# Output tiles in groups of 4, 1 and 4, and another listed order, in chunk attention followed by token mixing

## The chip, the cores and the metric

The kernel runs on one core of a Trainium2 chip. Its engines are PE (TensorE, matrix products), DVE (VectorE), ACT (ScalarE), POOL (GpSimd) and SP (SyncE); the DMA engines move data between device memory and the on-chip SBUF. PE writes to PSUM, which has 8 banks of 512 float32 columns here. The metric is the device time of one execution in microseconds (us), lower is better.

## The reference

`q`, `k` and `v` are 8 batches x 8 heads x 576 rows x 64 columns, float32. The attention is local: rows in chunks of 64, each chunk attends only to itself.

```
scores = q_c @ k_c.T / 8              # 64 x 64 for each of 8 * 8 * 9 = 576 chunks
attn   = exp(scores - max) / sum
x      = (attn @ v_c), heads side by side     # 8 x 576 x 512
wq, wk = x @ w_q, x @ w_k             # 8 x 576 x 64
mixed  = (wq @ wk.T / 8) @ x          # per batch, 576 x 576 never needed as such
out    = relu(mixed) @ w_out          # 8 x 576 x 512, float32
```

The kernel works in float16 and uses `(wq @ wk.T) @ x = wq @ (wk.T @ x)`, so that the middle is a 64 x 512 matrix G of each batch.

## The kernel before

One long list, `ORDER` (lines 17 to 45), says in which order everything is issued. A word is a step, a number (unit, batch or tile), for some a part behind a dot, the PSUM bank behind `@`, and the engine behind `:` (A for ACT, D for DVE, P for POOL). The loop at line 434 issues the words one after another. Each engine, and each engine's DMA queue, keeps its own words in the order of the list and waits where it needs data or a free buffer; nothing else sets the order. So a word far ahead in the list can hold up what follows it on the same engine and no other.

The work comes in **units** and **batches**. A unit is 32 chunks of `q` and `k`; there are 18, and a batch of 72 chunks takes two and a quarter. The steps of a unit:

- `LDu.q..`, `LDu.k..` (lines 147, 151): loads by POOL's queue, float32 to float16, in pieces. `q13` is one unit's fourth quarter of rows, `q21` the middle half of two units, `k2` the k of two units. In float16 a unit has 256 KB of k and 256 KB of q. `CQg` (159, 161) clears, once, the places of q that no load fills.
- `TRu` (203): DVE transposes q, or q and k. `KNu` makes the other layout of k: with `:D` by a further DVE transpose (207), and then TR takes two slices; with `:P` by a POOL copy (212) of the third slice of TR.
- `SCu` (223): 32 products for the scores; `EXu` (232): ACT's exponential.

The steps of a batch b:

- `LDb.v..` (142): v, in groups of chunks; `v09` is all of it, 576 KB in float16; `v04`, `v49`, `v05` and `v59` are parts.
- `PVb.p` (254), p = 0 to 3: attention times v for two heads, with the sums in a further column. `RNb.p` (266, 267): DVE divides, giving x.
- `XTb.0`, `XTb.1` (277): PE transposes x; `XE` (291, 293) evicts it. `XTb` needs all four RN of the batch.
- `PJb` (303): x times w_q and w_k; `EP` evicts (314, 316), `DU` (320) copies a part to the other half of the partitions.
- `WTb` (325) transposes wk, `EW` (330, 332) evicts; `GMb` (338) forms G, `EG` (348, 350) evicts; `MXb.m` (356), m = 0 to 3, forms wq @ G for half of the rows and half of the columns, `RL` (370, 372) applies the relu into the tile `rmx`.

`rmx` holds two batches side by side: 1152 rows, nine output tiles of 128 rows. `OMn` (397), n = 0 to 35, is the product of one tile with w_out, `OEn` (409, 411) evicts it. `LW` (166) loads w_out, 512 KB, in four DMAs on POOL's queue.

The tiles of a pair are gathered in groups, listed in `HOMES` (376): a group of size s takes s * 128 rows of the pair, and its tile r takes every s-th row, starting at r (line 396), so that each partition holds s whole rows in a line. Only when all rows of a group are mixed can any of its tiles be formed. When the last tile of a group is evicted, one store by SP's queue (415) writes the group. The evicted tiles lie in places of `qk` whose units are transposed by then; the second number of an entry of `HOMES` is that place, of 36.

SP's queue issues the stores in the order in which the list completes the groups. The first store also waits for the last load but one (`after`, line 508), so that loads and stores don't mix for most of the time. `ZZ` (424) is a matmul on constant data, whose result nobody uses; it keeps PE active.

Of the kernel before, what the change touches and what calls it, by code (L numbers as in the profile page):

```python
# [14 lines left out]
PSUM = bass.MemoryType.PSUM  # L15

ORDER = """
CQ7:A CQ1:D MU ZZ1@0 ZZ1@1 ZZ1@2 ZZ1@3 LS LD1.k1 LD1.q13 LD1.q10 CQ2:D CQ0:D MV LD1.q11 TR1 ZZ1@4 ZZ1@5 ZZ1@6 ZZ3@7
ZZ1@0 ZZ1@5 CQ4:A ZZ1@1 CQ6:A CQ3:A CQ5:A KN1:D LD2.q13 LD2.q11 LD2.k1 LD2.q10 TR2 LD0.k1 LI ZZ1@3 SC1@0 ZZ1@7
KN2:D SC2@4 ZZ1@7 ZZ1@3 ZZ1@7 LD0.q11 LD0.q10 LD0.q13 TR0 KN0:D SC0@2 EX1 EX2 LD0.v49 LD3.q23 PV0.3@6 PV0.2@4 RN0.2  # L20
LD0.v04 LD3.q20 EX0 PV0.1@0 RN0.1 PV0.0@2 LY:A ZZ1@4 RN0.0 ZZ3@5 RN0.3 LD3.k2 LD3.q21 XT0.1@3 TR4 XT0.0@7 XE0.0:A
LD5.q20 KN4:D SC4@0 XE0.1:A PJ0@6 EX4 EP0:A ZZ1@2 TR3 KN3:D SC3@2 DU0:D WT0@6 EW0:D LD1.v09 PV1.0@4 RN1.0 EX3
PV1.2@6 GM0@3 RN1.2 PV1.1@4 RN1.1 LD5.q23 PV1.3@0 EG0:A MX0.2@6 RL0.2:A MX0.1@2 RL0.1:A RN1.3 XT1.0@4 XE1.0:A
LD5.q21 XT1.1@5 XE1.1:A MX0.0@2 RL0.0:A MX0.3@0 PJ1@5 RL0.3:A LD5.k2 TR6 KN6:D TR5 KN5:D SC6@2 EP1:A EX6 DU1:D
WT1@7 EW1:D SC5@5 EX5 LD2.v09 PV2.3@0 RN2.3 LW OM1@3 OE1:A PV2.2@6 RN2.2 PV2.0@4 RN2.0 GM1@2 EG1:A PV2.1@0 OM2@3
OE2:A MX1.0@6 MX1.1@4 RL1.1:A RN2.1 LD7.q21 LD7.k2 OM0@2 RL1.0:D XT2.1@0 OE0:A XE2.1:A XT2.0@5 XE2.0:A LD7.q23
LD7.q20 LD9.k2 LD9.q21 LD9.q23 OM5@4 OE5:A MX1.3@2 RL1.3:A MX1.2@6 RL1.2:A TR7 KN7:D SC7@0 LD9.q20 EX7 PJ2@4 OM4@2
OE4:A OM3@6 OE3:A OM8@0 TR8 KN8:D OE8:A LD3.v09 LD11.q10 LD11.q11 EP2:D WT2@4 EW2:A LD12.q23 OM7@2 OE7:A TR9 TR10
SC8@6 PV3.1@3 RN3.1 LD4.v09 LD11.q13 LD11.k1 LD12.q20 PV3.0@0 RN3.0 DU2:P GM2@2 EX8 PV3.3@6 RN3.3 EG2:A MX2.1@2
RL2.1:A PV3.2@4 RN3.2 MX2.3@0 RL2.3:A KN9:P SC9@2 EX9 LD12.q21 MX2.0@6 RL2.0:D LD12.k2 LD14.q20 OM6@0 OE6:D XT3.1@4  # L30
XE3.1:A KN10:P LD14.q23 XT3.0@1 XE3.0:A MX2.2@6 RL2.2:A PV4.0@2 RN4.0 SC10@4 EX10 PJ3@0 EP3:A OM9@6 OE9:A LD14.q21
LD14.k2 TR11 PV4.1@2 RN4.1 PV4.2@4 RN4.2 LD5.v09 DU3:D KN11:P WT3@0 EW3:A OM12@1 GM3@0 LD16.q23 SC11@6 OE12:A
LD16.q20 TR12 EG3:A MX3.0@2 MX3.2@0 EX11 RL3.0:A LD6.v09 OM10@5 RL3.2:A OE10:A PV4.3@6 RN4.3 OM11@4 MX3.1@2 RL3.1:A
MX3.3@0 TR13 KN12:P TR14 SC12@6 LD16.q21 XT4.0@5 XT4.1@2 RL3.3:A OM14@0 OE14:D XE4.0:A XE4.1:A EX12 TR15 OM13@5
OE13:A OM15@2 OE15:A KN13:P OE11:A PJ4@0 EP4:A LD7.v59 PV5.1@6 RN5.1 PV5.0@2 RN5.0 SC13@4 EX13 PV5.2@0 WT4@6 EW4:A
RN5.2 OM16@7 KN14:P PV5.3@2 OE16:A RN5.3 SC14@4 EX14 GM4@6 XT5.0@1 DU4:P EG4:D MX4.1@6 RL4.1:D MX4.3@2 XE5.0:A
MX4.2@4 RL4.2:A OM17@0 OE17:D RL4.3:A KN15:P XT5.1@6 XE5.1:A MX4.0@4 RL4.0:D PV6.1@2 RN6.1 SC15@0 EX15 PV6.0@6
RN6.0 PJ5@4 EP5:A DU5:D OM19@2 OE19:A PV6.3@0 RN6.3 PV6.2@5 LD16.k2 WT5@4 EW5:A OM18@3 LD7.v05 OE18:A GM5@7 EG5:A
RN6.2 XT6.0@2 XE6.0:A TR16 KN16:P MX5.1@6 RL5.1:D MX5.0@0 RL5.0:A XT6.1@3 XE6.1:A OM20@2 MX5.2@0 RL5.2:A OE20:A
MX5.3@5 TR17 KN17:P RL5.3:D SC16@3 EX16 OM22@7 OE22:D PJ6@0 EP6:A PV7.0@4 RN7.0 PV7.1@2 SC17@6 DU6:P RN7.1 EX17  # L40
WT6@0 EW6:A OM23@1 OE23:A PV7.3@6 RN7.3 PV7.2@4 RN7.2 GM6@0 EG6:A OM21@1 OE21:A MX6.2@2 RL6.2:D MX6.1@6 RL6.1:A
XT7.1@4 XE7.1:D XT7.0@1 OM25@0 XE7.0:A PJ7@4 OE25:D OM24@7 EP7:A WT7@3 EW7:D MX6.3@4 RL6.3:D MX6.0@0 RL6.0:A GM7@2
EG7:D OE24:A DU7:D OM28@5 MX7.3@6 OE28:A MX7.1@1 MX7.0@3 OM29@0 OE29:D OM27@5 RL7.3:D OE27:D RL7.1:A RL7.0:A OM30@1
OM31@0 OE31:A OE30:D OM32@5 OE32:D MX7.2@6 RL7.2:A OM26@3 OE26:A OM33@6 OE33:A OM34@4 OE34:A OM35@1 ZZ1@6 OE35:A
""".split()


# [491 lines left out]
```

## Time and profile before

| | |
|---|---|
| median of 3 runs | 119.21 us (117.7 to 119.91) |
| the profiled execution: its own time | 118.41 us |
| its span, first to last instruction | 116.5 us |
| mean granted PE clock | 0.952 |
| busy: PE / DVE / ACT / POOL | 95.2 / 84.7 / 74.4 / 55.7 us |
| loads (POOL's queue) | 14.68 MB written to SBUF |
| output (SP's queue) | 17 stores: 7 of 768 KB, 5 of 512 KB, 5 of 256 KB |

The span is shorter than the execution's time, which has what lies around the first and last instruction too. A granted clock of 1.00 is full speed. A row of a view of groups reads: line, engine, operation, output <- input, shape, count | busy us, mean ns of one | idle time before, and what ended it. A row of the timeline reads: start, length, engine, line, operation, count, and in brackets the idle time before it and what ended that. Matmuls overlap with those ahead and behind, so a row of the chain that ended last (start, length, what) prices a group of matmuls better than the length in the timeline.

### The profile page before, as it was taken

To read this page: it belongs to the slowest core of one execution; us is meant where nothing else is said; L and a number is where in the kernel's file an instruction comes from. 1 tells how busy PE (TensorE), PEld (TensorE's weight loads), DVE (VectorE), ACT (ScalarE), POOL (GpSimd) and SP (SyncE) were. 2 spreads that over 40 slices of the span, in tenths; PEclk is the share of its full clock that TensorE was granted. 3 is DMA by queue.
4 is the path that set the end of the run, shared out by engine and by line. 5 is a ranking of instruction groups with operands and counts; after the bars stand their busy time and mean duration, and the time that the engine had idled before them with its cause. 6 is when DMAs were issued, how large, how long until landed. Compare 5 with 4: busy or idle time off the path is not lost.

```text
span 116.5 us, 3850 instructions
## 1 busy us (share of the span) xinstructions
PE 95.2 (82%) x1648; PEld 53.8 (46%) x1648; DVE 84.7 (73%) x135; ACT 74.4 (64%) x109; POOL 55.7 (48%) x77
## 2 busy tenths in 40 slices
...
GB/s 31 187 177 198 160 172 211 178 168 211 173 176 203 211 214 197 164 182 162 200 213 207 203 165 174 161 179 190 114 264 407 400 407 400 295 191 7 371 385 143
DMA packets 46016, 24.62 MB, mean 211 GB/s; under 512 B 38192, under 2 KB 39216, under 8 KB 46000
## 3 DMA queue, kind: packets, MB, share of 16 engines
q0 software_dynamic: 42912, 14.68, 113.0%
...
q14 instruction: 3, 0.02, 0.1%
...
## 4 chain that ended last, share of the span: by engine, by line
DMA 50%; PE 26%; POOL 9%; DVE 7%; issue 4%; ACT 1%; DVEq 0%; POOLq 0%
DMA vt<-in_v_dram 43%; PE pb L397 13%; DMA qk<-in_k_dram 7%; POOL qk L151 5%; PE pb L303 3%; DVE qkT L203 3%; POOL qk L147 2%; PE pb L338 2%; PE pb L277 2%; PE pb L254 2%; PE pb L356 2%; DVE xn L267 1%; PE pb L223 1%; DVE rmx L370 1%; POOL vt L142 1%
## 5 line engine op out<-in xcount | busy, mean ns | idle before, releaser
L397 PE MATMUL pb<-wout,rmx 128*128 128x512 f16 x144 | 35.7, 380 | 0.1
L203 DVE STREAM_TRANSPOSE qkT<-qk 128x1536 f32<-128x1536 f32 (+2 forms) x20 | 26.9, 1359 | 4.9 <-DMA qk<-in_q_dram 4.8
L267 DVE TENSOR_TENSOR xn<-pb,rec 128x576 f16<-128x576 f32 x32 | 24.2, 757 | 1.3 <-DVE rec L266 0.2
L232 ACT ACTIVATE est<-pb 128x1024 f16<-128x1024 f32 x18 | 18.5, 1026 | 9.9 <-PE pb L223 9.8
L151 POOL DMA_DIRECT2D qk<-in_q_dram x33 | 17.9, 548 | 10.3 <-DMA vt<-in_v_dram 6.0
L411 ACT COPY qk<-pb 128x512 f32<-128x512 f32 x27 | 15.8, 587 | 9.7 <-PE pb L397 9.1
L223 PE MATMUL pb<-qkT,kN 64*64 64x128 f16 x576 | 13.4, 235 | 7.4 <-DVE kN L207 7.3
L397 PEld LDWEIGHTS <-rmx 128*128 128x128 f16 x144 | 13.0, 101 | 13.1 <-DVE rmx L370 0.8
L142 POOL DMA_DIRECT2D vt<-in_v_dram x10 | 16.1, 1612 | 2.6 <-DMA qk<-in_k_dram 2.3
L212 POOL COPY kN<-qkT 128x512 int32<-128x512 int32 x9 | 9.7, 1083 | 14.5 <-DVE qkT L203 12.8
L372 ACT ACTIVATE rmx<-pb 128x576 f16<-128x576 f32 x23 | 14.3, 653 | 3.2 <-PE pb L356 2.2
L223 PEld LDWEIGHTS <-kN 64*64 64x64 f16 x576 | 10.4, 117 | 11.2 <-DVE kN L207 9.6
L293 ACT COPY xT<-pb 128x512 f32<-128x512 f32 (+1 forms) x15 | 9.2, 637 | 7.7 <-PE pb L277 7.6
L277 PE MATMUL pb<-iden,xn 128*128 128x128 f32 x72 | 9.9, 278 | 3.3 <-DVE xn L267 3.3
L266 DVE RECIPROCAL rec<-pb 128x9 f32<-128x9 f32 x32 | 6.8, 213 | 6.5 <-PE pb L254 6.5
L254 PE MATMUL pb<-vt,est 64*64 64x65 f16 x576 | 9.4, 194 | 2.2 <-DMA vt<-in_v_dram 1.8
L424 PE MATMUL pb<-unit 128*128 128x512 f16 x24 | 9.0, 516 | 2.6 <-DVE unit L448 2.6
L303 PE MATMUL pb<-xT,wpj 128*128 128x512 f16 (+1 forms) x64 | 10.4, 308 | 0.5 <-ACT xT L293 0.4
L277 PEld LDWEIGHTS pb<-iden,xn 128*128 128x128 f32 x72 | 7.9, 140 | 5.5 <-issue 2.6
L254 PEld LDWEIGHTS <-est 64*64 64x64 f16 x576 | 7.3, 107 | 5.8 <-ACT est L232 2.4
L207 DVE STREAM_TRANSPOSE kN<-qk 128x512 f32<-128x512 f32 x9 | 9.0, 1004 | 0.0
L409 DVE COPY qk<-pb 128x512 f32<-128x512 f32 x9 | 6.1, 683 | 4.0 <-PE pb L397 4.0
...
## 6 DMA issues: line engine op xcount, KB each, us to landing
...
qk<-in_q_dram POOLq DMA_DIRECT2D x7, 256.0 KB, 9.9
out_dram<-qk SPq DMA_DIRECT2D x5, 256.0 KB, 2.7
qk<-in_k_dram POOLq DMA_DIRECT2D x4, 256.0 KB, 6.0
```

The lines of the kernel that those rows point to most:

```text
L142: d = nc.gpsimd.dma_start(vt[b % NVB][:, lo:hi, 0:D], vb[b, :, lo:hi])
L151: d = nc.gpsimd.dma_start(view[rows, SIDE[i], j : j + n], qt[rows, b : b + n])
L203: nc.vector.transpose(out=to[:, s : s + step], in_=words(view[:, s : s + step, j]))
L223: nc.tensor.matmul(ps[CH * (eta % 2) : CH * (eta % 2) + CH, bank + f, P * g : P * g + P], lhsT=kN[u % NR][rows, CH * eta : CH * eta + CH, ...
L232: nc.scalar.activation(est[u % NR][:].rearrange("p f g k (w r) -> p (f g k) w r", r=R), ps[:, bank : bank + 2].rearrange("p k c -> p (k c) ...
L254: nc.tensor.matmul(ps[CH * o : CH * o + CH, bank + at // 512, at % 512 : at % 512 + D + 1], lhsT=est[u % NR][rows, i // 2, eta // 2, SIDE[i]],
L267: nc.vector.tensor_tensor(out=xn[b % 3][:, :, p], in0=xv[:, :, 0:D], in1=rec[p][:, :, None].broadcast_to([P, NPR, D]), op=ALU.mult,)
L277: nc.tensor.transpose(ps[:, bank + at // 4, P * (at % 4) : P * (at % 4) + P], xn[b % 3][:, i].rearrange("p h c -> p (h c)").bitcast(F32), ...
L303: nc.tensor.matmul(to, lhsT=wpj[:, c, e, :], rhs=rhs, start=(c == 0 and e == 0), stop=(c == 1 and e == 1),)
L372: nc.scalar.activation(dst, src, AF.Relu, scale=scale_moe)
L397: nc.tensor.matmul(ps[:, bank, :], lhsT=c[:, r], rhs=wout[:, i, :], start=(i == 0), stop=(i == NI - 1),)
L411: nc.scalar.copy(os_, ps[:, bank, :])
```

## The change

`HOMES` and `ORDER` change; no function does. In pairs 0 and 1 the groups of output tiles are 4, 1, 4 instead of 3, 3, 3 and 3, 1, 3, 2. A group of four tiles has 512 rows, so the first one of a pair lies within its first batch of 576 rows; the single one spans both batches. In pair 2 they are 2, 2, 1, 2, 2 instead of 2, 2, 2, 2, 1, and in pair 3 they are 2, 2 and five single ones instead of 3, 3 and three single ones. That gives 18 stores: 4 of 1024 KB, 6 of 512 KB, 8 of 256 KB.

The list has the same steps, in another order, with other banks, and on other engines in places: KN is DVE's in 12 units instead of 9, OE in 5 tiles instead of 9, RL in 7 instead of 9, XE in 4 instead of 1, EP in 3 instead of 1, EG in 1 instead of 2, and DU in 2 batches instead of 5 (the rest of KN and DU is POOL's, of the others ACT's). The whole of it:

```diff
@@ -15,33 +15,33 @@
 PSUM = bass.MemoryType.PSUM
 
 ORDER = """
-CQ7:A CQ1:D MU ZZ1@0 ZZ1@1 ZZ1@2 ZZ1@3 LS LD1.k1 LD1.q13 LD1.q10 CQ2:D CQ0:D MV LD1.q11 TR1 ZZ1@4 ZZ1@5 ZZ1@6 ZZ3@7
-ZZ1@0 ZZ1@5 CQ4:A ZZ1@1 CQ6:A CQ3:A CQ5:A KN1:D LD2.q13 LD2.q11 LD2.k1 LD2.q10 TR2 LD0.k1 LI ZZ1@3 SC1@0 ZZ1@7
-KN2:D SC2@4 ZZ1@7 ZZ1@3 ZZ1@7 LD0.q11 LD0.q10 LD0.q13 TR0 KN0:D SC0@2 EX1 EX2 LD0.v49 LD3.q23 PV0.3@6 PV0.2@4 RN0.2
-LD0.v04 LD3.q20 EX0 PV0.1@0 RN0.1 PV0.0@2 LY:A ZZ1@4 RN0.0 ZZ3@5 RN0.3 LD3.k2 LD3.q21 XT0.1@3 TR4 XT0.0@7 XE0.0:A
-LD5.q20 KN4:D SC4@0 XE0.1:A PJ0@6 EX4 EP0:A ZZ1@2 TR3 KN3:D SC3@2 DU0:D WT0@6 EW0:D LD1.v09 PV1.0@4 RN1.0 EX3
-PV1.2@6 GM0@3 RN1.2 PV1.1@4 RN1.1 LD5.q23 PV1.3@0 EG0:A MX0.2@6 RL0.2:A MX0.1@2 RL0.1:A RN1.3 XT1.0@4 XE1.0:A
-LD5.q21 XT1.1@5 XE1.1:A MX0.0@2 RL0.0:A MX0.3@0 PJ1@5 RL0.3:A LD5.k2 TR6 KN6:D TR5 KN5:D SC6@2 EP1:A EX6 DU1:D
-WT1@7 EW1:D SC5@5 EX5 LD2.v09 PV2.3@0 RN2.3 LW OM1@3 OE1:A PV2.2@6 RN2.2 PV2.0@4 RN2.0 GM1@2 EG1:A PV2.1@0 OM2@3
-OE2:A MX1.0@6 MX1.1@4 RL1.1:A RN2.1 LD7.q21 LD7.k2 OM0@2 RL1.0:D XT2.1@0 OE0:A XE2.1:A XT2.0@5 XE2.0:A LD7.q23
-LD7.q20 LD9.k2 LD9.q21 LD9.q23 OM5@4 OE5:A MX1.3@2 RL1.3:A MX1.2@6 RL1.2:A TR7 KN7:D SC7@0 LD9.q20 EX7 PJ2@4 OM4@2
-OE4:A OM3@6 OE3:A OM8@0 TR8 KN8:D OE8:A LD3.v09 LD11.q10 LD11.q11 EP2:D WT2@4 EW2:A LD12.q23 OM7@2 OE7:A TR9 TR10
-SC8@6 PV3.1@3 RN3.1 LD4.v09 LD11.q13 LD11.k1 LD12.q20 PV3.0@0 RN3.0 DU2:P GM2@2 EX8 PV3.3@6 RN3.3 EG2:A MX2.1@2
-RL2.1:A PV3.2@4 RN3.2 MX2.3@0 RL2.3:A KN9:P SC9@2 EX9 LD12.q21 MX2.0@6 RL2.0:D LD12.k2 LD14.q20 OM6@0 OE6:D XT3.1@4
-XE3.1:A KN10:P LD14.q23 XT3.0@1 XE3.0:A MX2.2@6 RL2.2:A PV4.0@2 RN4.0 SC10@4 EX10 PJ3@0 EP3:A OM9@6 OE9:A LD14.q21
-LD14.k2 TR11 PV4.1@2 RN4.1 PV4.2@4 RN4.2 LD5.v09 DU3:D KN11:P WT3@0 EW3:A OM12@1 GM3@0 LD16.q23 SC11@6 OE12:A
-LD16.q20 TR12 EG3:A MX3.0@2 MX3.2@0 EX11 RL3.0:A LD6.v09 OM10@5 RL3.2:A OE10:A PV4.3@6 RN4.3 OM11@4 MX3.1@2 RL3.1:A
-MX3.3@0 TR13 KN12:P TR14 SC12@6 LD16.q21 XT4.0@5 XT4.1@2 RL3.3:A OM14@0 OE14:D XE4.0:A XE4.1:A EX12 TR15 OM13@5
-OE13:A OM15@2 OE15:A KN13:P OE11:A PJ4@0 EP4:A LD7.v59 PV5.1@6 RN5.1 PV5.0@2 RN5.0 SC13@4 EX13 PV5.2@0 WT4@6 EW4:A
-RN5.2 OM16@7 KN14:P PV5.3@2 OE16:A RN5.3 SC14@4 EX14 GM4@6 XT5.0@1 DU4:P EG4:D MX4.1@6 RL4.1:D MX4.3@2 XE5.0:A
-MX4.2@4 RL4.2:A OM17@0 OE17:D RL4.3:A KN15:P XT5.1@6 XE5.1:A MX4.0@4 RL4.0:D PV6.1@2 RN6.1 SC15@0 EX15 PV6.0@6
-RN6.0 PJ5@4 EP5:A DU5:D OM19@2 OE19:A PV6.3@0 RN6.3 PV6.2@5 LD16.k2 WT5@4 EW5:A OM18@3 LD7.v05 OE18:A GM5@7 EG5:A
-RN6.2 XT6.0@2 XE6.0:A TR16 KN16:P MX5.1@6 RL5.1:D MX5.0@0 RL5.0:A XT6.1@3 XE6.1:A OM20@2 MX5.2@0 RL5.2:A OE20:A
-MX5.3@5 TR17 KN17:P RL5.3:D SC16@3 EX16 OM22@7 OE22:D PJ6@0 EP6:A PV7.0@4 RN7.0 PV7.1@2 SC17@6 DU6:P RN7.1 EX17
-WT6@0 EW6:A OM23@1 OE23:A PV7.3@6 RN7.3 PV7.2@4 RN7.2 GM6@0 EG6:A OM21@1 OE21:A MX6.2@2 RL6.2:D MX6.1@6 RL6.1:A
-XT7.1@4 XE7.1:D XT7.0@1 OM25@0 XE7.0:A PJ7@4 OE25:D OM24@7 EP7:A WT7@3 EW7:D MX6.3@4 RL6.3:D MX6.0@0 RL6.0:A GM7@2
-EG7:D OE24:A DU7:D OM28@5 MX7.3@6 OE28:A MX7.1@1 MX7.0@3 OM29@0 OE29:D OM27@5 RL7.3:D OE27:D RL7.1:A RL7.0:A OM30@1
-OM31@0 OE31:A OE30:D OM32@5 OE32:D MX7.2@6 RL7.2:A OM26@3 OE26:A OM33@6 OE33:A OM34@4 OE34:A OM35@1 ZZ1@6 OE35:A
+MU CQ4:A LS LD0.k1 CQ0:D LD0.q10 ZZ1@0 ZZ1@1 ZZ1@2 ZZ1@3 ZZ1@4 CQ7:D LD0.q11 CQ6:D ZZ1@5 LD0.q13 LD1.k1 ZZ1@6 ZZ1@7
+ZZ1@3 ZZ1@6 ZZ1@4 MV ZZ1@2 TR0 KN0:D CQ1:A LD1.q11 LD1.q10 ZZ1@2 CQ2:A CQ3:A LY:A LD1.q13 LD2.q13 ZZ1@2 SC0@4 TR1
+KN1:D ZZ1@0 ZZ1@2 ZZ5@0 SC1@1 LD2.q11 LD2.k1 LD2.q10 TR2 KN2:D SC2@6 LI LD0.v04 EX0 CQ5:A EX1 PV0.0@3 RN0.0 LD0.v49
+PV0.1@2 RN0.1 LD3.q21 LD3.k2 PV0.2@0 RN0.2 ZZ2@4 EX2 ZZ1@4 PV0.3@6 RN0.3 XT0.0@5 XE0.0:A LD3.q20 LD3.q23 TR3 KN3:D
+XT0.1@0 XE0.1:A PJ0@0 EP0:A DU0:D SC3@4 WT0@1 EX3 EW0:D TR4 GM0@3 EG0:A MX0.0@6 MX0.1@2 LD5.q20 MX0.3@0 RL0.0:A
+LD1.v09 MX0.2@4 RL0.2:A PV1.0@6 RL0.3:D KN4:D LW PV1.2@0 RN1.2 RN1.0 SC4@4 RL0.1:A EX4 LD5.q23 PV1.1@2 LD5.q21
+PV1.3@4 OM0@0 RN1.1 OE0:A OM3@6 OE3:A RN1.3 XT1.0@2 XE1.0:A LD5.k2 XT1.1@4 XE1.1:A OM2@3 OE2:A TR5 PJ1@4 EP1:A
+KN5:D SC5@0 EX5 WT1@7 TR6 KN6:D LD2.v09 PV2.1@2 RN2.1 SC6@0 EW1:A PV2.0@5 RN2.0 LD7.q20 GM1@4 LD7.q23 LD7.q21
+LD7.k2 EX6 PV2.3@0 RN2.3 LD9.q20 LD3.v09 PV2.2@2 LD9.q23 DU1:P EG1:A MX1.1@6 RL1.1:A OM1@4 OE1:A RN2.2 MX1.0@0
+RL1.0:A MX1.2@5 RL1.2:A XT2.0@2 XE2.0:A XT2.1@3 XE2.1:A OM4@7 MX1.3@5 RL1.3:A TR7 KN7:D SC7@0 TR8 KN8:D PJ2@3 EP2:D
+OE4:A EX7 OM5@5 OE5:A DU2:D SC8@6 EX8 PV3.0@0 RN3.0 LD9.k2 LD9.q21 PV3.1@2 RN3.1 WT2@4 EW2:A OM7@5 PV3.3@6 RN3.3
+OE7:A GM2@4 EG2:A MX2.0@3 RL2.0:A MX2.1@5 RL2.1:A LD11.q11 LD11.q13 OM6@7 OE6:A PV3.2@2 TR9 LD11.k1 MX2.2@0 MX2.3@4
+RL2.3:A RL2.2:A RN3.2 LD4.v09 OM8@6 LD11.q10 XT3.0@2 XE3.0:A LD12.q20 LD12.q21 LD14.q20 LD12.k2 KN9:P SC9@3 XT3.1@0
+OM12@5 EX9 TR10 XE3.1:A KN10:D OE12:A SC10@2 EX10 OE8:D TR11 PV4.0@0 KN11:D RN4.0 PJ3@6 EP3:A OM9@5 OE9:A WT3@4
+PV4.1@6 RN4.1 LD12.q23 LD14.q23 SC11@2 PV4.2@0 RN4.2 LD14.q21 LD14.k2 LD5.v09 EW3:A GM3@4 EX11 PV4.3@6 DU3:P EG3:A
+MX3.3@4 RL3.3:A MX3.1@2 RL3.1:A OM11@0 OE11:A RN4.3 XT4.1@5 XT4.0@2 XE4.1:A TR12 MX3.2@3 RL3.2:A MX3.0@0 OM10@7
+RL3.0:A LD6.v09 LD16.q23 LD16.k2 OE10:A LD16.q20 XE4.0:D PJ4@5 EP4:A KN12:P SC12@0 EX12 LD16.q21 OM16@3 WT4@5 EW4:A
+TR13 LD7.v59 KN13:P OE16:A OM15@6 OE15:A GM4@2 EG4:A SC13@4 EX13 TR14 DU4:P TR15 KN14:P KN15:P PV5.2@0 RN5.2
+PV5.0@6 RN5.0 OM17@2 OE17:A SC14@3 PV5.1@0 RN5.1 OM14@5 LD7.v05 PV5.3@6 EX14 MX4.1@2 RL4.1:A MX4.3@0 RL4.3:A OM13@4
+RN5.3 OE14:D MX4.0@2 RL4.0:A MX4.2@6 RL4.2:D XT5.1@0 OE13:A XE5.1:D XT5.0@5 XE5.0:A SC15@6 EX15 PV6.1@2 PV6.0@0
+RN6.1 PJ5@4 RN6.0 EP5:A DU5:P OM21@2 OE21:A WT5@4 EW5:A TR16 OM20@0 PV6.3@1 RN6.3 OE20:A PV6.2@5 GM5@3 OM18@4 EG5:A
+MX5.2@0 OE18:A RL5.2:A RN6.2 MX5.0@2 RL5.0:D XT6.1@6 XT6.0@5 XE6.0:A MX5.1@2 RL5.1:A KN16:P SC16@0 EX16 MX5.3@4
+RL5.3:A XE6.1:D PJ6@6 OM22@2 TR17 KN17:D SC17@0 EX17 PV7.0@3 OE22:A EP6:D WT6@6 RN7.0 OM24@5 EW6:D PV7.2@0 DU6:P
+RN7.2 PV7.3@3 RN7.3 OE24:A PV7.1@6 RN7.1 GM6@2 EG6:A OM23@5 OE23:A OM19@2 MX6.0@0 OE19:A RL6.0:D MX6.2@4 XT7.0@6
+XT7.1@2 XE7.1:D RL6.2:A MX6.1@0 RL6.1:D MX6.3@4 OM26@7 XE7.0:A PJ7@2 EP7:D DU7:P OE26:A OM27@7 OE27:D OM28@0 OE28:A
+WT7@2 EW7:D RL6.3:A OM25@7 GM7@2 OM29@0 EG7:D OE25:A MX7.2@3 MX7.3@1 OE29:A RL7.2:D MX7.1@5 RL7.1:D OM30@7 OE30:D
+MX7.0@3 RL7.3:A OM34@1 OE34:D RL7.0:A OM33@4 OE33:A OM31@6 OE31:A OM32@5 OE32:A OM35@3 OE35:A
 """.split()
 
 
@@ -374,10 +374,10 @@
     of = out.rearrange("b s m -> (b s) m")
     ring = words(qk[:])
     HOMES = (
-        ((3, 0), (3, 3), (3, 6)),
-        ((3, 27), (1, 30), (3, 31), (2, 34)),
-        ((2, 9), (2, 11), (2, 13), (2, 15), (1, 17)),
-        ((3, 18), (3, 21), (1, 24), (1, 25), (1, 26)),
+        ((4, 0), (1, 4), (4, 5)),
+        ((4, 27), (1, 31), (4, 32)),
+        ((2, 9), (2, 11), (1, 13), (2, 14), (2, 16)),
+        ((2, 18), (2, 20), (1, 22), (1, 23), (1, 24), (1, 25), (1, 26)),
     )
 
     done = {}
```

## The prediction

> **What bounds the kernel now.** I read the stretches first, then the chain that ended last, then the durations by form. Columns of the stretches: from:to, length, busy time (and instructions) of PE, PEld, DVE, ACT, POOL, then granted clock, DMA share, GB/s.
>
> ```profile
> span 116.5 us, 3850 instructions
> ...
> 12.00:39.00 27.00, 17.34 (x376) 11.14 (x376) 19.73 (x32) 11.44 (x18) 14.10 (x21) 0.81 1.71 185
> 39.00:73.50 34.50, 33.66 (x624) 19.61 (x621) 31.14 (x43) 27.59 (x45) 24.98 (x29) 1.00 1.62 190
> 73.50:86.70 13.20, 12.68 (x317) 8.14 (x317) 10.80 (x22) 9.47 (x15) 3.67 (x4) 1.00 1.71 171
> 86.70:112.80 26.10, 25.50 (x290) 12.52 (x288) 15.75 (x25) 15.50 (x27) 2.80 (x3) 1.00 0.80 318
> ```
>
> From 39 us on, PE is busy 71.84 of 73.8 us. Before that it is not: 17.34 of 27 us, at a mean granted clock of 0.81. So the end is set by how much PE work is left when PE becomes full, and by whatever stops it later. The chain that ended last (start, length, what) names the one thing that does, and also gives PE's price for each word of the list, at full clock:
>
> ```profile
> 19.62 17.21 DMA vt<-in_v_dram
> ...
> 59.64 13.90 DMA vt<-in_v_dram
> ...
> 76.74 0.46 PE pb L223 x32
> 77.20 0.78 PE pb L338 x10
> ...
> 80.64 0.23 PE pb L356 x2
> ...
> 93.11 0.44 PE pb L325 x6
> ...
> 94.41 0.44 PE pb L254 x35
> ...
> 96.95 1.13 PE pb L277 x9
> ...
> 98.09 0.86 PE pb L397 x4
> 98.95 1.02 PE pb L303 x8
> ...
> 112.23 0.58 ACT qk L411
> ```
>
> Prices: SC 0.46, GM 0.78, MX 0.23, WT 0.44, PV 0.23 (35 matmuls are two words), both XT of a batch 1.13, OM 0.86, PJ 1.02. The load issued at 59.64 is v of batch 5 (LD5.v09), landing at 73.54. PE stood for it:
>
> ```profile
> 73.58 0.48 PE L254 MATMUL pb<-vt,est 64*64 64x65 f16 x34 [0.40 <-DMA vt<-in_v_dram]
> ```
>
> And from the DMA views of single stretches, the last load and the last stores (for issues: KB, us to landing; for the queues: start, length):
>
> ```profile
> vt<-in_v_dram POOLq DMA_DIRECT2D x1, 320.0 KB, 10.3
> ...
> 76.43 1.30 POOL L142 DMA_DIRECT2D vt<-in_v_dram  x1
> ...
> 111.97 0.33 SPq L415 DMA_DIRECT2D out_dram<-qk  x1
> ...
> 112.84 0.33 SPq L415 DMA_DIRECT2D out_dram<-qk  x1
> ...
> out_dram<-qk SPq DMA_DIRECT2D x1, 256.0 KB, 2.3
> ```
>
> So PE reaches the list's PV5 just as v5 lands: **the load stream and PE meet at 73.5 us**, which I call the gate. Behind it, PE runs until 112.2, evicts (0.58), stores (issued at 112.84, landed 2.3 later), and closes. The last load, issued at 76.43, lands 10.3 later, at 86.7, and PE still has 25.5 us of work then. Its PV7 stand later in the list, so that load binds nothing.
>
> **The change part by part.** Work is moved, not removed: both lists hold 18 SC, 32 PV, 8 each of PJ, WT, GM, 8 pairs of XT, 32 MX, 36 OM, the same 54 loads, and 24 warming matmuls (ZZ).
>
> *Early part.* Where two lists have the same kinds of work, I compare their reach when the gates open.
>
> ```profile
> 23.24 1.25 DVE L203 STREAM_TRANSPOSE qkT<-qk 128x1024 f32<-128x1024 f32 x1 [1.33 <-DMA qk<-in_q_dram]
> 23.26 1.18 ACT L293 COPY xT<-pb 128x512 f32<-128x512 f32 x2 [4.67 <-PE pb L277]
> 26.46 2.10 PE L303 MATMUL pb<-xT,wpj 128*128 128x512 f16 x8
> 39.97 0.40 PE L397 MATMUL pb<-wout,rmx 128*128 128x512 f16 x1
> ```
>
> Before, the units are taken 1, 2, 0; after, 0, 1, 2. By then 3136 KB of loads must have landed for the fourth unit in either list, so its transpose stays at about 23.2 (summing the loads' sizes in listed order). PJ0 has its input at 23.26 + 1.18 = 24.44 but starts at 26.46, as SC4 stands ahead of it in PE's queue and needs that transpose; after, PJ0 stands ahead of SC3. Batch 0's mixing (PJ, WT, GM, MX) thus starts about 2 us sooner, and the weights wout (LW) are loaded before units 5 and 6 instead of after v2. With four output tiles over the first 512 of batch 0's 576 rows, OM0, OM3 and OM2 can run before batch 1 is mixed. Before, the first OM is at 39.97, behind 7 SC, 9 PV, 2 XT pairs, 2 PJ, 2 WT, 1 GM, 4 MX. After, ahead of SC6, stand 6 SC, the same rest, and 3 OM: 3 x 0.86 - 0.46 = **2.12 us of work gained** if both get there at one time. Against it: LW's 512 KB now delay units 5, 6 and v2. From v2's landing (19.62 + 17.21 = 36.83, after 5312 KB) and the 23.24 above (3136 KB) the stream does 160 KB/us, so they come up to 3.2 us later than before; units 5, 6 had, by the same rate, 36.83 - 576 / 160 = 33.2, so at most 36.4, where the DVE is still busy with batch 1's four RN. I count 0.6 us of loss (between nothing and 1.5): PE's lead is about 1.5 us at 40 us.
>
> Some of the ZZ that stood between 19 and 29 us move ahead of SC1. By the row 12 to 39 the clock is 0.81 there, and PJ0 takes 2.10 us against 1.02 later. If the three OM met that half speed, they would cost 3 x 0.86 more, 2.6 us, and the early lead would be gone; the row from 39 on has 1.00, and OM0 stands behind a dense run of batches 0 and 1, so nothing is my value and 2.6 the other end. [...]
>
> *At the gate.* Loads up to v5 and with it come to 12160 KB in both lists, and the queue stood full (DMA share 1.62 over 39 to 73.5), so it lands at 73.5 again; plus or minus 1, since the order of q pieces differs. Ahead of the first PV5 the old list has 13 SC, 20 PV, 5 XT, 5 PJ, 4 WT, 4 GM, 16 MX, 16 OM. The new one has 14 SC, 20 PV, 5 XT, 5 PJ, 5 WT, 5 GM, 16 MX, 15 OM. The difference: 0.46 + 0.44 + 0.78 - 0.86 = **0.82 us more work ahead of the gate**. Before, PE came 0.4 us ahead of v5; now it comes 0.4 + 1.5 - 0.82 = 1.1 ahead, and waits that long. So of the early gain only 0.82 survives, as less work behind the gate.
>
> *Engines.* Moves between engines, by form:
>
> ```profile
> L267 DVE TENSOR_TENSOR xn<-pb,rec 128x576 f16<-128x576 f32 x32 | 24.2, 757 | 1.3 <-DVE rec L266 0.2
> L203 DVE STREAM_TRANSPOSE qkT<-qk 128x1536 f32<-128x1536 f32 x9 | 15.7, 1759 | 0.0
> L207 DVE STREAM_TRANSPOSE kN<-qk 128x512 f32<-128x512 f32 x9 | 9.0, 1004 | 0.0
> L203 DVE STREAM_TRANSPOSE qkT<-qk 128x1024 f32<-128x1024 f32 x7 | 8.5, 1220 | 3.5 <-DMA qk<-in_q_dram 3.5
> L266 DVE RECIPROCAL rec<-pb 128x9 f32<-128x9 f32 x32 | 6.8, 213 | 6.5 <-PE pb L254 6.5
> L370 DVE TENSOR_SCALAR rmx<-pb 128x576 f16<-128x576 f32 x9 | 6.7, 745 | 0.8 <-PE pb L356 0.8
> L409 DVE COPY qk<-pb 128x512 f32<-128x512 f32 x9 | 6.1, 683 | 4.0 <-PE pb L397 4.0
> L320 DVE COPY wq<-wqk 64x576 f16<-64x576 f16 x5 | 1.6, 327 | 2.1 <-ACT wqk L316 1.9
> L291 DVE COPY xT<-pb 128x640 int32<-128x640 int32 x1 | 0.8, 824 | 0.0
> L314 DVE CAST wqk<-pb 128x576 f16<-128x576 f32 x1 | 0.8, 757 | 0.0
> ...
> L411 ACT COPY qk<-pb 128x512 f32<-128x512 f32 x27 | 15.8, 587 | 9.7 <-PE pb L397 9.1
> L372 ACT ACTIVATE rmx<-pb 128x576 f16<-128x576 f32 x23 | 14.3, 653 | 3.2 <-PE pb L356 2.2
> L293 ACT COPY xT<-pb 128x640 f32<-128x640 f32 x7 | 4.9, 693 | 1.0 <-PE pb L277 1.0
> L316 ACT CAST wqk<-pb 128x576 f16<-128x576 f32 x7 | 4.5, 638 | 3.6 <-PE pb L303 3.6
> ```
>
> DVE: three KN more, 3 x (1.004 + 1.220 - 1.759) = +1.40; four OE less, -2.73; two RL less, -1.49; three XE more, two of them at 0.824 and one at the 512-wide copy's 0.683, +2.33; two EP, +1.51; three DU less, -0.98; one EG less, at most -0.68. In all between -0.6 and 0. ACT: four OE, +2.35; two RL, +1.31; three XE less, about -1.97 (two at 0.693, one at 0.587); two EP less, -1.28; the EG at most +0.59: some +0.4 to +1.0. On POOL three KN copies less and three DU more; it has room (24.98 of 34.5). DVE is nearly as full as PE (31.14 of 34.5), so a neutral sum matters: no new bound, and I take nothing for it.
>
> *Stores.* 17 become 18, the last five tiles each alone. Both lists end in OM, OE, one 256 KB store, so the closing 0.58 + 2.3 and the rest stay.
>
> **Sum.** 118.41 (the profiled execution: span 116.5 and 1.9 around it) - 0.82 = 117.6. The median shown, 119.21, lies 0.8 above that execution, so in its terms **118.4**. Gaps behind the gate: 38.66 us from 73.54 to 112.2, for 81.0 - 43.7 = 37.3 of work by the prices, so 1.3; I keep them.
>
> **Rivals.**
>
> *A: the gate opens early, and the lead is kept.* If the new load order brings v5 at 72 or sooner, PE keeps its lead of 1.5 and the old wait of 0.4 goes: 119.21 - 1.9 = 117.3; with no early loss (2.12) 116.7, and with half of the 1.3 us of gaps gone 116.0. For it: POOL's KN copies stand between fewer of the loads. Against: a full queue is not helped by earlier issue.
>
> *B: slower, by TR16.* In the new list DVE's queue has RN6.1, RN6.0, TR16, RN6.3, RN6.2, and XT6 needs the last. TR16 needs LD16.q21, behind 13760 KB of loads. From 12160 KB at 73.54 and 14336 at 86.7 the stream does 165 KB/us there: 73.54 + 1600 / 165 = 83.2. TR16 and two RN follow before XT6.1: 1.76 + 2 x (0.757 + 0.213) = 3.7, so 86.9. PE reaches XT6.1 some 12.8 us of work behind the gate, at 86.3 to 86.8. So it decides from a landing at about 83.0, and each us later costs one: at the old last landing, 86.7, +3.7 - 0.8, 122.1. Before, TR16 stood behind all of RN6. POOL's KN12 ahead of LD16.q21 speaks for it, the full queue against.
>
> *C: the filler is missing.* Three OM spent early can't cover the evictions between PJ, WT, GM, MX in the batches that follow. Each such batch has EP 0.638 and RL 0.653 and their like uncovered, some 2 us. One is paid by the lead; a second and third give 119.2 + 2 to 3, 121 to 122.
>
> *D: stores in a row.* If each of the five single stores waited for the one ahead, five times the 2.3 of the row would stand behind the first, and most of the tail's OM with them: some +6, 124 to 125. The last store issues 0.87 behind the one ahead of it (112.84 against 111.97) and still lands in 2.3, so they overlap; I hold this for nearly excluded. [...]
>
> *E: no change*, 119.2: the gate's 0.82 is given back in gaps.
>
> **How the numbers follow.** Forecast 0.45 (117.3 to 119.0), A 0.18, B 0.20, C 0.10, D 0.02, E 0.05. 2% of 119.21 is 2.4 us, about what a measurement of this kernel can tell, as its three runs spread from 117.7 to 119.91. Faster by over 2% (under 116.8): over half of A, 0.13. Slower (over 121.6): half of B, C and D, 0.22. Within: 0.65. The range leaves out A's extreme and the worst of B, C, D: 115.9 to 122.0.
>
> **What would show it.** An OM before 36 us; PE idle for some 1.1 us at about 73.5, ended by the v load; the last OM's end at 111.4 instead of 112.2. TR16 waiting for a q load beyond 83 would be B; PE's busy time of 39 to 73.5 falling below 33, C. Wrong would be: v5 landing elsewhere than 72.5 to 74.5, or PE gaps behind the gate over 2 us in all.

## The result, and the profile after

The changed kernel is slower by about 1%.

| | before | after |
|---|---|---|
| median (20 runs each) | 118.47 us | 120.27 us |
| range | 117.68 to 120.41 | 118.62 to 122.93 |
| ratio, 95% interval | | 1.0106 [1.0073, 1.0140] |
| span of the profiled execution | 116.5 us | 117.4 us |
| mean granted PE clock in it | 0.952 | 0.936 |
| last OM's end | 112.23 | 113.46 |

Of the changed kernel's 20 runs, 9 took 120.4 to 122.9 us, eight of them at a mean granted clock under 0.91; the ratio leaves these out, and so is smaller than that of the medians, as the ratios below leave out such runs (7 of 12 each of the changed kernel with OM30 elsewhere and with single tiles, at most a third of any other kernel's).

The stretches of the changed kernel (columns as in the prediction: from:to, length, busy time of PE, PEld, DVE, ACT, POOL, granted clock, DMA share, GB/s):

```profile
12.00:39.00 27.00, 20.02 (x355) 11.58 (x348) 20.07 (x32) 12.68 (x17) 17.01 (x22) 0.78 1.68 180
39.00:73.50 34.50, 32.51 (x659) 19.57 (x658) 29.14 (x42) 28.23 (x46) 21.71 (x28) 1.00 1.63 189
73.50:86.70 13.20, 13.20 (x315) 7.79 (x313) 11.49 (x19) 10.22 (x17) 5.22 (x6) 1.00 1.67 175
```

Before 39 us PE is busy for 2.7 us more than it was, at a lower clock, 0.78. From 39 to 73.5 it is busy for 1.15 us less: it waits there. Single rows tell both. The timeline of PE up to that point:

```profile
24.02 2.08 PE L303 MATMUL pb<-xT,wpj 128*128 128x512 f16 x8 [0.78 <-ACT xT L293]
...
29.65 0.29 PE L356 MATMUL pb<-wqk,g 64*128 64x288 f16 x1 [0.47 <-ACT g L350]
...
33.83 0.35 PE L254 MATMUL pb<-vt,est 64*64 64x65 f16 x18 [1.03 <-ACT est L232]
34.11 3.54 PE L397 MATMUL pb<-wout,rmx 128*128 128x512 f16 x8
37.49 1.15 PE L277 MATMUL pb<-iden,xn 128*128 128x128 f32 x9
...
42.53 0.64 PE L223 MATMUL pb<-qkT,kN 64*64 64x128 f16 x31
```

PJ0 is at 24.02 (26.46 before), the first MX at 29.65, and OM0 at 34.11, all as early as forecast. But the eight matmuls of OM0 and OM3 take 3.38 us from their start to that of XT1 at 37.49, twice the 0.86 per word that the prediction had. SC6, the word by which the prediction counts PE's lead, is at 42.53. The stretches around it show why:

```profile
28.00:34.00 6.00, 3.19 (x122) 2.24 (x122) 5.08 (x10) 3.70 (x6) 3.92 (x5) 1.00 1.20 204
34.00:37.30 3.30, 3.30 (x26) 1.31 (x16) 3.27 (x5) 0.59 (x1) 3.16 (x4) 0.51 2.41 162
```

From 28 to 34 PE is busy for 3.19 of 6 us, with many short waits. Then the clock is 0.51 for 3.3 us, just where the OM that were to be the gain stand.

PE's waits from there to the gate, its total in the view of waits from 39 to 73.5 (engine, what it worked on, what it waited for: total, times, longest), and PE at batch 5's PV:

```profile
PE pb L254 <- ACT est L232: 1.0, 3, 0.5
PE pb L356 <- DVE xn L267: 0.5, 1, 0.5
PE pb L277 <- DVE xn L267: 0.4, 1, 0.4
PE pb L325 <- ACT wqk L316: 0.2, 1, 0.2
...
74.94 0.23 PE L254 MATMUL pb<-vt,est 64*64 64x65 f16 x4
```

That is 2.1 us of waits. (At 55.43, the 0.5 of line 356, the view names DVE, but the eviction of G on ACT, 0.37 us from 55.00, ends just ahead of it.) Before, in the same stretch, there was one wait:

```profile
PE pb L223 <- DVE kN L207: 0.2, 1, 0.2
```

The v5 load lands where it did. Its issue in the timeline, and its time to landing in the DMA view of that microsecond:

```profile
61.24 1.83 POOL L142 DMA_DIRECT2D vt<-in_v_dram  x1
...
vt<-in_v_dram POOLq DMA_DIRECT2D x1, 576.0 KB, 12.5
```

61.24 + 12.5 = 73.74. PE is at its PV at 74.94, without a wait for the load: 1.2 us behind v5, where it had been 0.4 ahead.

Behind the gate, the timelines of PE, ACT and DVE near the end:

```profile
106.38 0.39 PE L397 MATMUL pb<-wout,rmx 128*128 128x512 f16 x1
107.15 1.06 PE L397 MATMUL pb<-wout,rmx 128*128 128x512 f16 x3 [0.39 <-DVE rmx L370]
108.14 0.29 PE L356 MATMUL pb<-wqk,g 64*128 64x288 f16 x1
...
108.95 4.48 PE L397 MATMUL pb<-wout,rmx 128*128 128x512 f16 x20 [0.51 <-ACT rmx L372]
...
106.34 1.42 DVE L370 TENSOR_SCALAR rmx<-pb 128x576 f16<-128x576 f32 x2 [0.87 <-PE pb L356]
...
108.25 1.19 ACT L372 ACTIVATE rmx<-pb 128x576 f16<-128x576 f32 x2 [1.66 <-PE pb L397]
...
113.46 0.59 ACT L411 COPY qk<-pb 128x512 f32<-128x512 f32 x1 [0.28 <-PE pb L397]
```

OM30 (106.38) stops after its first matmul until RL7.2 and RL7.1 have written (DVE, 106.34), and RL7.3 on ACT (108.25) starts only when OM30 is through. Neither is needed for a result: OM30 takes every second one of the rows 256 to 511 of its pair, all of batch 6, and RL7 writes batch 7. The built program has these waits: OM30's second and fourth weight loads wait for RL7.2 and RL7.1 (0.68 and 0.55 us in PEld's timeline, at 107.15 and 107.81), RL7.3 for OM30's last matmul (the 1.66 above). The view of waits from 74.9 to 113.5 has the two weight loads (PEld):

```profile
PEld L397 <- DVE rmx L370: 1.2, 2, 0.7
```

In the kernel before, RL7.1 and RL7.0 wait for their MX alone.

### The profile page after: what moved, and what is told of

Read it like the earlier page. It is cut to its first block, busy times and chain, and to the rows that moved or that the text cites. A ratio compares the mean times of both kernels' runs of the same rounds, so it can differ in the third digit from the quotient of the medians.

```text
span 117.4 us, 3858 instructions
## 1 busy us (share of the span) xinstructions
PE 98.0 (84%) x1648; PEld 54.4 (46%) x1648; DVE 84.9 (72%) x133; ACT 73.8 (63%) x111; POOL 54.3 (46%) x77
## 4 chain that ended last, share of the span: by engine, by line
PE 60%; DMA 12%; DVE 11%; POOL 5%; ACT 5%; issue 3%; DVEq 0%; POOLq 0%; ACTq 0%
PE pb L397 28%; DMA qk<-in_q_dram 12%; PE pb L223 7%; PE pb L277 7%; PE pb L303 7%; PE pb L356 4%; DVE xn L267 4%; PE pb L254 4%; PE pb L338 3%; ACT est L232 3%; PE pb L325 2%; DVE rmx L370 2%; POOL qk L151 2%; DVE kN L207 2%; POOL vt L142 1%
## 5 line engine op out<-in xcount | busy, mean ns | idle before, releaser
L397 PE MATMUL pb<-wout,rmx 128*128 128x512 f16 x144 | 38.1, 395 | 1.0 <-ACT rmx L372 0.5
L203 DVE STREAM_TRANSPOSE qkT<-qk 128x1024 f32<-128x1024 f32 (+2 forms) x20 | 25.3, 1279 | 5.1 <-DMA qk<-in_q_dram 5.1
L411 ACT COPY qk<-pb 128x512 f32<-128x512 f32 x31 | 18.0, 588 | 13.7 <-PE pb L397 13.7
L397 PEld LDWEIGHTS <-rmx 128*128 128x128 f16 x144 | 13.5, 107 | 14.7 <-issue 3.8
L372 ACT ACTIVATE rmx<-pb 128x576 f16<-128x576 f32 x25 | 15.3, 652 | 4.4 <-PE pb L356 2.5
L320 POOL COPY wq<-wqk 64x576 f16<-64x576 f16 x6 | 4.0, 663 | 26.3 <-DVE wqk L314 14.4
L207 DVE STREAM_TRANSPOSE kN<-qk 128x512 f32<-128x512 f32 x12 | 12.2, 1013 | 0.0
L424 PE MATMUL pb<-unit 128*128 128x512 f16 x24 | 9.8, 581 | 1.5 <-DVE unit L448 1.5
L293 ACT COPY xT<-pb 128x512 f32<-128x512 f32 (+1 forms) x12 | 7.4, 637 | 5.1 <-PE pb L277 5.0
L212 POOL COPY kN<-qkT 128x512 int32<-128x512 int32 x6 | 6.5, 1093 | 4.7 <-PE pb L254 3.3
```

Of the source, the lines that this page charges most:

```text
L203: nc.vector.transpose(out=to[:, s : s + step], in_=words(view[:, s : s + step, j]))
L372: nc.scalar.activation(dst, src, AF.Relu, scale=scale_moe)
L397: nc.tensor.matmul(ps[:, bank, :], lhsT=c[:, r], rhs=wout[:, i, :], start=(i == 0), stop=(i == NI - 1),)
L411: nc.scalar.copy(os_, ps[:, bank, :])
```

## The experiments

All ratios are to the kernel before on the same chip, 95% interval behind. Two numbers of a profiled execution are followed through them: the time at which PE starts batch 5's PV (73.58 before, 74.94 after), and the time from there to the last OM's end, "the tail" (112.23 - 73.58 = 38.65 before, 113.46 - 74.94 = 38.52 after).

### Keep the clock up

```diff
-EW0:D TR4 GM0@3 EG0:A MX0.0@6
+EW0:D TR4 ZZ2@7 GM0@3 EG0:A ZZ2@7 MX0.0@6
...
-RN1.2 RN1.0 SC4@4
+RN1.2 RN1.0 ZZ2@5 SC4@4
...
-PV1.1@2 LD5.q21 PV1.3@4
+PV1.1@2 ZZ4@0 LD5.q21 PV1.3@4
```

> The kernel after, with ten more idle matmuls in PE's gaps between 28 and 34 us, so that the clock is not at half speed when the two first output tiles come. If the half clock is what cost the early lead: OM0 and OM3 take 0.86 us each instead of 1.74, PJ1 starts near 37.7 us instead of 39.4, PE reaches PV5 at about the landing of v5 (73.7), and the time falls by 1.2 us to a ratio to before of 0.998 to 1.003. If it is only the place of the output tiles ahead of XT1, and not the clock: less than 0.5 us.

Ratio 1.0058 [1.0021, 1.0095]. The same two stretches, and the timeline of PE:

```profile
28.00:34.00 6.00, 5.51 (x118) 2.79 (x115) 4.86 (x9) 3.77 (x6) 5.44 (x7) 1.00 1.30 201
34.00:37.30 3.30, 3.30 (x37) 2.35 (x37) 3.23 (x7) 1.60 (x4) 1.66 (x2) 1.00 2.33 171
...
34.46 1.92 PE L397 MATMUL pb<-wout,rmx 128*128 128x512 f16 x8
...
73.92 0.23 PE L254 MATMUL pb<-vt,est 64*64 64x65 f16 x4
```

With ten idle matmuls in the waits, the clock holds at 1.00, OM0 and OM3 together take 1.92 instead of 3.54, and PE is at batch 5's PV at 73.92, 1.02 us sooner, though it does more (v5 lands at 60.80 + 12.7 = 73.5). The tail stays at 112.45 - 73.92 = 38.53. So the half clock costs about 0.5% by the runs (1.0106 against 1.0058) and 1.02 us, 0.9%, by these two executions, and is not the whole loss. The two intervals overlap, and 1.0058 lies between the two forecasts: the runs alone leave the size open, from nothing to 1%. That the clock is the cause rests on the rows.

### The three early OM later

Undoes the part that was to give the gain: OM0, OM3 and OM2 go behind GM1, PV2.2 and MX1.3.

```diff
-PV1.3@4 OM0@0 RN1.1 OE0:A OM3@6 OE3:A RN1.3
+PV1.3@4 RN1.1 RN1.3
...
-XE1.1:A OM2@3 OE2:A TR5
+XE1.1:A TR5
...
-LD7.k2 EX6 PV2.3@0
+LD7.k2 OM0@7 EX6 OE0:A PV2.3@0
...
-EG1:A MX1.1@6
+EG1:A OM3@5 OE3:A MX1.1@6
...
-MX1.3@5 RL1.3:A TR7
+MX1.3@5 OM2@2 RL1.3:A OE2:A TR7
```

> The kernel after, with OM0, OM3 and OM2 moved behind GM1, PV2 and MX1.3, so that XT1, PJ1 and SC5 don't stand behind them. If their place is what starved DVE (3.25 us idle before PV2): PJ1 near 36 us, DVE idle under 1.5 us there, the three tiles fill PE's gaps between 42 and 47, and the time falls by 1 to 2 us, ratio 0.995 to 1.003. If only the clock counted, the three tiles are paid later at full speed and the gain is 0 to 0.7 us, ratio 1.005 to 1.011.

Ratio 1.0463 [1.0420, 1.0506], by far the slowest kernel of the study, and outside both forecasts. Two stretches:

```profile
34.00:36.00 2.00, 0.35 (x18) 0.23 (x17) 1.93 (x6) 0.32 (x1) 1.23 (x2) 0.72 2.46 159
36.00:44.00 8.00, 6.67 (x90) 4.76 (x94) 4.20 (x6) 3.31 (x5) 2.03 (x4) 0.50 1.50 194
```

Where the early OM had been, PE is idle for 1.65 of 2 us, and the clock then stays at 0.50 for 8 us. So the early OM, slow as they run, also keep PE at work; without them in this order, far more is lost. The undoing takes more away than the one thing, so it prices the hole, and not the OM.

### OM30 elsewhere in the list

```diff
-EG7:D OE25:A MX7.2@3 MX7.3@1 OE29:A RL7.2:D MX7.1@5 RL7.1:D OM30@7 OE30:D MX7.0@3 RL7.3:A
+EG7:D OE25:A OM30@7 MX7.2@3 MX7.3@1 OE29:A RL7.2:D MX7.1@5 RL7.1:D RL7.3:A OE30:D MX7.0@3
```

> The kernel after, with OM30 ahead of MX7 and of RL7 in the list, nothing else. If the waits of OM30 for batch 7's RL (0.39 us) and of RL7.3 for OM30 (OM34 0.51 us later) are what lengthens the tail: the last OM ends 0.4 to 0.9 us sooner, ratio 1.003 to 1.007. If those waits only hide another one: unchanged at 1.0106.

Ratio 1.0067 [1.0018, 1.0117]. In PE's timeline OM30 runs through, but the next word takes over the wait:

```profile
108.11 0.28 PE L356 MATMUL pb<-wqk,g 64*128 64x288 f16 x1 [0.70 <-DVE rmx L370]
```

MX7.0 needs the bank that RL7.2 empties, and nothing stands between them any more. The tail is 112.86 - 75.03 = 37.83, 0.69 shorter, within the forecast. But the interval takes in nearly the whole way from no gain to the tail's full price, so this run alone settles nothing.

### The groups alone, in the kernel before

The kernel before with the new `HOMES`; its list changes only in that OM3 and OM5 swap places, with their evictions, so that each group is complete in time.

```diff
-((3, 18), (3, 21), (1, 24), (1, 25), (1, 26)),
+((2, 18), (2, 20), (1, 22), (1, 23), (1, 24), (1, 25), (1, 26)),
```

(and the other three pairs as in the change)

> The kernel before, with only the new groups of output tiles (tiles 3 and 5 change places in the list, since tile 5 now needs all of batch 1). If the size and number of the stores have no price of their own, as the prediction took: ratio 0.997 to 1.003. If single stores at the end cost their fixed time in a row: slower by 2 us or more, ratio above 1.015.

Ratio 1.0111 [1.0070, 1.0151]: as much as the whole change, with the old order. PE is at batch 5's PV at 73.63, but the last OM ends at 113.22, a tail of 39.59 for 38.65. ACT's timeline, of this kernel and of the one before:

```profile
105.60 1.19 ACT L372 ACTIVATE rmx<-pb 128x576 f16<-128x576 f32 x2 [1.72 <-PE pb L397]
```

```profile
104.02 1.20 ACT L372 ACTIVATE rmx<-pb 128x576 f16<-128x576 f32 x2
```

RL7.1 and RL7.0 start 1.58 us later, behind OM27, which as part of a group of two lies in rows 0 to 255 of its pair, batch 6 again. On PE, OM30 then stands for them:

```profile
106.30 0.38 PE L397 MATMUL pb<-wout,rmx 128*128 128x512 f16 x1 [0.74 <-ACT rmx L372]
...
106.85 2.55 PE L397 MATMUL pb<-wout,rmx 128*128 128x512 f16 x11 [0.17 <-ACT rmx L372]
```

These two waits, 0.91 us, are the tail's 0.94. In this execution the span also ends 5.3 us behind the last OM's end, for 4.3 before; what makes that was not followed up.

### Only pair 3's groups: of three, or single

Two kernels, each that of the last section with another pair 3.

```diff
-((2, 18), (2, 20), (1, 22), (1, 23), (1, 24), (1, 25), (1, 26)),
+((3, 18), (3, 21), (1, 24), (1, 25), (1, 26)),
```

> The kernel before with the new groups of 4 and 1 in pairs 0 to 2, and the old groups of 3 and its single tiles in pair 3 alone. Theory (the groups cost only by the waits between tile 27's reads and RL7.1's write in pair 3): RL7.1 begins at 104.0 again, the last OM ends at 112.2, ratio 0.997 to 1.003. Rival (larger groups and other store sizes cost by themselves, everywhere): ratio stays at 1.008 to 1.014.

```diff
-((2, 18), (2, 20), (1, 22), (1, 23), (1, 24), (1, 25), (1, 26)),
+tuple((1, i) for i in range(18, 27)),
```

> The kernel before with the new groups in pairs 0 to 2 and nine groups of one tile in pair 3 (20 stores instead of 15). Theory (the wait comes from reads in steps of two columns, which take in columns of the other batch): a group of one reads in steps of one, RL7.1 begins at 104.0, ratio 0.997 to 1.003. Rival (each store has a fixed price at the end, and nine small ones in a row cost about 0.3 us each beyond what is hidden): last OM's end at 112.2 but the span longer by 1 to 2 us, ratio 1.008 to 1.017.

With the old groups of three in pair 3: 0.9985 [0.9948, 1.0022]; with nine single ones: 0.9968 [0.9937, 1.0000]. ACT's rows, of the one and of the other:

```profile
103.10 1.20 ACT L372 ACTIVATE rmx<-pb 128x576 f16<-128x576 f32 x2
```

```profile
104.13 1.20 ACT L372 ACTIVATE rmx<-pb 128x576 f16<-128x576 f32 x2
```

In both, RL7.1 waits for no OM. (Of the 0.92 us by which the first is ahead of the kernel before, 0.64 begin earlier: PE is at batch 5's PV at 72.94 in that execution.) Their tails are 111.31 - 72.94 = 38.37 and 112.33 - 73.97 = 38.36, after 38.65 before. So groups of four and their 1024 KB stores cost nothing measurable, nor do 20 stores instead of the 17 before (the expectation says 15); that each store has a fixed time or price, as two rivals in the expectations suppose, no run shows. Of the new groups, only the groups of two in pair 3 cost anything measurable, and the waits are what the profile shows of it. An OM of a group of two reads every second column of `rmx`, and an RL writes a part of two of its four rows at once, the first two or the last two. The weight loads that wait are those of the second row of each two: they lie between the two parts of such a write, and touch neither. Why the built program holds reads in steps of two to overlap it, and those in steps of three and of one not, these runs don't show.

### Single tiles in pair 3 of the changed kernel

The same edit of pair 3, in the changed kernel, with its list untouched.

> The changed kernel with pair 3 in nine groups of one tile, its list untouched. Theory (the tail's share of the loss is the wait of OM30 for RL7.2 and RL7.1 and of RL7.3 for OM30, and it goes with the reads in steps of two): PE still reaches PV5 at 74.9, the last OM's end comes 0.6 to 0.8 us sooner, at 112.7 to 112.9, ratio 1.003 to 1.006. Rival (OM30 would be late anyway, by its bank or by its eviction): last OM's end at 113.4, ratio 1.009 to 1.013.

Ratio 1.0012 [0.9973, 1.0051]. PE is at batch 5's PV at 74.94, as before this edit. The end of its timeline, and ACT's rows:

```profile
106.39 1.04 PE L397 MATMUL pb<-wout,rmx 128*128 128x512 f16 x4
107.36 0.29 PE L356 MATMUL pb<-wqk,g 64*128 64x288 f16 x1
...
107.59 4.49 PE L397 MATMUL pb<-wout,rmx 128*128 128x512 f16 x20
...
106.50 0.66 ACT L372 ACTIVATE rmx<-pb 128x576 f16<-128x576 f32 x1
107.70 0.65 ACT L372 ACTIVATE rmx<-pb 128x576 f16<-128x576 f32 x1 [0.54 <-PE pb L356]
```

OM30 takes 1.04 without a stop, and the last twenty matmuls start at 107.59 instead of 108.95. The last OM ends at 112.11: a tail of 37.17, 1.35 us shorter. That is twice what I expected. I had gone by PE's idle times of 0.39 and 0.51, and these don't show all of it: from OM30's start to MX7.0 it had been 108.14 - 106.38 = 1.76 us for 0.97 now, and from there to the next OM 0.81 for 0.23.

### Both causes together

The idle matmuls and a new tail, in which RL6.3 moves ahead of PJ7, OM30 takes the place of OM25 behind WT7, and OM25 that of OM30:

```diff
-EW7:D RL6.3:A OM25@7 GM7@2
+EW7:D OM30@7 GM7@2
...
-RL7.1:D OM30@7 OE30:D MX7.0@3
+RL7.1:D OM25@7 OE25:D MX7.0@3
```

> The changed kernel with the idle matmuls of the run with the clock kept up, and with its tail laid out anew: OM30 ahead of WT7's successor GM7, where RL6.3 (moved ahead of PJ7) is its only late input, and OM25 as the filler between MX7.1 and MX7.0. Theory (two causes: half clock at OM0 and OM3 costs about 1 us of the 1.1% and the false waits behind OM30 about 0.6 to 0.8 us): last OM ends at 111.4 to 111.8, span 115.4 to 115.8, ratio to the kernel before 0.996 to 1.002. Rival (the groups' stores or the order by itself cost something at the end that neither edit reaches): the last OM is sooner as said, but the span stays above 116.3 and the ratio above 1.004. Rival (clock and tail are the same slack told twice): ratio 1.005 to 1.007 as with either edit alone.

Ratio 0.9961 [0.9926, 0.9995]: PV at 73.96, last OM's end 111.17, tail 37.21, a little better than the sizes I had given the two causes. Without the new tail, but with single tiles in pair 3, and with all three edits:

> The changed kernel with the idle matmuls of the run with the clock kept up, and pair 3 in nine groups of one tile; its list otherwise untouched. Theory (the changed kernel's loss is two separate costs, 0.9% by the tail's waits and 0.5% by the half clock, on top of a gain of some 0.4%): they add, ratio 0.994 to 0.999, PE at PV5 at 73.9 to 74.0, last OM's end at 111.0 to 111.3. Rival (the two edits recover the same time): ratio 1.000 to 1.003.

> The kernel with both edits (clock kept up, tail laid out anew) and pair 3 in nine groups of one tile as well. Theory (with OM30 early no OM of a group of two stands near the last RL, so the groups cost nothing more): as the run without the new layout of the tail, last OM's end at 111.0 to 111.3, ratio 0.994 to 0.999. Rival (the moved OM25 or RL6.3 costs or gains by itself): the two differ by over 0.4 us in the last OM's end counted from PV5.

| kernel | ratio | PV of batch 5 | tail |
|---|---|---|---|
| after | 1.0106 [1.0073, 1.0140] | 74.94 | 38.52 |
| clock kept up | 1.0058 [1.0021, 1.0095] | 73.92 | 38.53 |
| single tiles | 1.0012 [0.9973, 1.0051] | 74.94 | 37.17 |
| clock, single tiles | 0.9965 [0.9923, 1.0007] | 74.68 | 37.10 |
| clock, new tail | 0.9961 [0.9926, 0.9995] | 73.96 | 37.21 |
| all three | 0.9932 [0.9889, 0.9975] | 73.57 | 37.10 |

The two costs add: 0.0048 by the clock and 0.0094 by the waits, 0.0142 in all, and 0.0141 measured for both. Each of these differences is uncertain by about 0.005, so that they agree to 0.0001 is luck. The rival, 1.000 to 1.003, lies at the upper end of the interval, 1.0007; what speaks against it are the rows, PV5 sooner by the one edit and a shorter tail by the other. Given single tiles, the new tail changes nothing in the tail's length (37.10 both). In the executions of the last two kernels with single tiles PE waits for v5 again, as in the kernel before; in the first of them v5 itself is late, so PV5 and the last OM's end, 111.78, miss the forecast of 73.9 to 74.0 and 111.0 to 111.3:

```profile
74.68 0.51 PE L254 MATMUL pb<-vt,est 64*64 64x65 f16 x36 [0.23 <-DMA vt<-in_v_dram]
```

```profile
73.57 0.51 PE L254 MATMUL pb<-vt,est 64*64 64x65 f16 x36 [0.51 <-DMA vt<-in_v_dram]
```

So with the clock kept up the gate can bind again; in the two other kernels with the idle matmuls (73.92, 73.96) PE still came a little behind v5. The kernel with all three edits is the only one that is faster than the kernel before by more than half a percent: 0.7%, by its interval between 0.2 and 1.1%.

### Two that decided nothing

One fills a wait ahead of the gate, in the kernel with clock and new tail: OM6 moves ahead of MX2.0.

```diff
-GM2@4 EG2:A MX2.0@3 RL2.0:A MX2.1@5 RL2.1:A LD11.q11 LD11.q13 OM6@7 OE6:A PV3.2@2
+GM2@4 EG2:A OM6@7 MX2.0@3 RL2.0:A OE6:A MX2.1@5 RL2.1:A LD11.q11 LD11.q13 PV3.2@2
```

> The kernel with both edits (clock kept up, tail laid out anew), and OM6 moved ahead of MX2.0, where PE stood 0.47 us at 54.15 for G. Theory (PE comes to v5 some 0.4 us after it has landed, so that time saved ahead of it is worth just that much): PE is at PV5 at 73.5 to 73.7 instead of 73.96, last OM's end 0.3 to 0.4 us sooner than with both edits alone, ratio 0.992 to 0.996. Rival (the eviction that PE waits for moves with it, or the next wait takes it over): PV5 at 73.9, ratio as with both edits alone, 0.996.

Ratio 1.0018 [0.9979, 1.0057], no better. PE's timeline shows the rival:

```profile
54.76 1.02 PE L397 MATMUL pb<-wout,rmx 128*128 128x512 f16 x4 [0.51 <-DVE xn L267]
56.76 0.34 PE L254 MATMUL pb<-vt,est 64*64 64x65 f16 x17 [0.48 <-ACT rmx L372]
57.79 0.28 PE L356 MATMUL pb<-wq,g 64*128 64x288 f16 x1 [0.34 <-ACT rmx L372]
```

OM6 stops for 0.51 itself, and two waits follow that were not there. PE came to the gate only at 75.47, partly because its first 40 us ran later in this execution.

The other puts ten idle matmuls into the kernel before:

```diff
-LD3.q21 XT0.1@3
+LD3.q21 ZZ4@2 XT0.1@3
...
-KN4:D SC4@0
+KN4:D ZZ6@2 SC4@0
```

> The kernel before with ten more idle matmuls, four ahead of XT0.1 and six ahead of SC4, so that its own stretch at half clock, 24 to 30 us, is shorter. Theory (before, PE waits at the gate for v5, so that time gained ahead of it is worth nothing): PJ0 near 1.1 us long instead of 2.10, PE idle ahead of PV5 grows from 0.4 to above 1 us, v5 at 73.5 as before, ratio 0.998 to 1.003. Rival (any half clock costs its own length, wherever it lies): last OM's end 0.8 to 1.5 us sooner, ratio 0.988 to 0.994.

Ratio 1.0018 [0.9983, 1.0054], as the theory had it, but not for its reason. PJ0 is at full speed, and the half clock comes later instead, over XT1 and PJ1 (mean granted clock 0.73 from 32 to 36 us and 0.68 from 36 to 38):

```profile
25.99 1.20 PE L303 MATMUL pb<-xT,wpj 128*128 128x512 f16 x8
...
33.45 1.83 PE L277 MATMUL pb<-iden,xn 128*128 128x128 f32 x9 [1.51 <-DVE xn L267]
36.06 1.74 PE L303 MATMUL pb<-xT,wpj 128*128 128x512 f16 x8 [0.18 <-ACT xT L293]
```

The lead was not gained, so the run says nothing of what one would be worth. It does show that here the slow stretch moved when waits ahead of it were filled: from 24 to 30 us the mean clock is 0.50 in the kernel before and 1.00 in this one.

## Why the prediction was wrong

The forecast was 0.8 us faster; it came out 1.1% slower, some 1.3 us. It is on the wrong side by two costs that the sum priced at nothing, a stretch at half clock and false waits near the end, and its account of how PE comes to the gate failed with them.

**Right.** *Early part*, the order of events: PJ0 2 us sooner (2.4), an OM before 36 us (34.11), and v2 at 40.0 (issued at 30.08, 9.9 to landing). *At the gate*: v5 at 73.74 for a forecast of 73.5. *Engines*: no new bound came of the moves. The sums there were not right: DVE is busy for 84.9 us after 84.7, for a forecast between 0.6 less and the same, and ACT for 73.8 after 74.4, for 0.4 to 1.0 more. They left out that the clearing of q (CQ) changes engines too, which the section on the change does not say either: ACT clears one place of 2048 columns less (1.89 us) and one of 1024 more (1.04). *Stores*: span end 3.9 us behind the last OM's end for 4.3 before; D is refuted by the kernel with 20 stores (0.9968). B is refuted too; DVE reaches TR16 in its turn, waits for nothing, and two RN follow:

```profile
84.03 1.77 DVE L203 STREAM_TRANSPOSE qkT<-qk 128x1536 f32<-128x1536 f32 x1
85.89 0.22 DVE L266 RECIPROCAL rec<-pb 128x9 f32<-128x9 f32 x1
```

**First failed step: "nothing is my value and 2.6 the other end"** in *Early part*, for three OM at half speed. Two of the three met it. I argued that OM0 stands behind a dense run of batches 0 and 1. A list that is dense in words is not dense in time: PE was busy for 3.19 of the 6 us ahead of it (the last section has the stretch that counts, and its share of 0.50). OM0 and OM3 lost 1.6 us (3.54 for 1.92 with the clock kept up); at the gate that is 1.02 us in these executions, and 0.5% of the time by the runs. The clock fell without a long idle window: the longest single wait between 28 and 34 is 1.03 us. It came back at 37.46, after 3.41 us, from 34.05 on, in which PE was busy without a stop.

**Second: "PE's lead is about 1.5 us at 40 us"**, and "waits that long" at the gate. By the prediction's own count the lead is 2.12 less the time by which SC6 (42.53) comes behind 39.97: -0.4 us, and, with the clock kept up, where SC6 is at 41.25, +0.8. PE's waits from 39 to 73.5, 2.1 us for 0.2 before, stand nowhere in the sum. They are rival C in small: PV stand close behind the EX that feed them, XT2 behind its RN, MX behind its EG. C priced 2 us for each batch; it was 2 us for all. The sign set for C did come, PE's busy time of 39 to 73.5 falling below 33 (32.51), and PE's idle 1.1 us at the gate did not. Forecast, PE came 1.1 us ahead of v5, at 72.4; measured, 74.94, which is 2.5 late, and these waits (1.9 more than before) with the clock (1.0) come to about that, 2.9. Of this only the 1.2 us behind v5 counted. With the clock kept up, PE was at the gate between 0.4 us behind v5 and 0.5 ahead of it, so these waits alone cost little; how much was not separated.

**Third: "Gaps behind the gate ... I keep them"**, and *Stores*, which looked at pair 3's groups only as stores. By the same prices the gaps were 38.52 us less 36.5 of work (37.3 less 0.82), 2.0 instead of 1.3, and without the groups of two 0.7. So the tail's waits cost 1.35 us in the profile and 0.9% in the runs, and this is the larger term. The groups are also what OM reads, in steps, and the step went with which writes it was held against: with steps of two, OM30's weight loads stood 0.68 and 0.55 us for RL7.2 and RL7.1; with steps of one, in the same list, OM30 took its 1.04 without a stop. I had no such wait among the rivals; "PE gaps behind the gate over 2 us in all" was in the text as a sign of being wrong, and 2.0 is just at its edge.

**The 0.82** of work moved ahead of the gate is there in the profile: with both costs gone the tail is 37.10, 1.55 us shorter than before, of which 0.82 would be work and 0.7 gaps by the prices. PE's busy time in the tail says much the same: 37.06 us for 38.00 before. The runs don't show it. With both costs gone they give 0.9965 [0.9923, 1.0007], and the old list with the same single tiles in pair 3 gives 0.9968 [0.9937, 1.0000], so that the new order by itself has no gain to show. Only the kernel with all three edits is lower, and its interval overlaps with both; that its 0.9932 is the forecast, 118.4 / 119.21 = 0.9932, is chance, for the forecast had none of the edits in it.
